# A convolution and a gated unit on one core: where the fourth product of two first stages stands, and how the last stores are cut

## The chip, the cores and the metric

The kernel runs on one core of one Trainium2 chip. The metric is the device time of one execution in microseconds (us), the median of several. A core has TensorE (PE in the profile, its weight loads apart as PEld), VectorE (DVE), ScalarE (ACT), GpSimd (POOL) and SyncE (SP). Each has its own queue of instructions in an order that is fixed when the program is built, and goes on only when the semaphores that its next instruction waits for are there. SP, ACT and POOL also issue the DMAs, which 16 DMA engines of the core carry out.

## What is computed

The input u has 2048 tokens of 448 channels. It is normalised over the channels, and two branches of the result are added to it: a long convolution, whose kernel is made from 256 complex states for each channel and applied by a Fourier transform of length 4096, and a gated unit.

```python
xn = _layernorm(u, axis=-1)
# branch A, for each channel
dt = exp(log_dt); A = -exp(log_A_real) + 1j * A_imag; C = (C_real + 1j * C_imag) * dt
K = 2 * einsum("dn,dnl->dl", C, exp(A * dt * pos)).real
y = irfft(rfft(xn, 4096) * rfft(K, 4096))[:2048] + xn * D_skip
# branch B, F = 1792
h = sigmoid(xn @ w_gate) * (xn @ w_up)
out = u + y + h @ w_down
```

## The kernel before

**Two generators, one order.** `conv()` (branch A) and `glu()` (branch B) are Python generators. A loop at the end of the kernel takes a step of one or of the other by the work that each has announced with `yield`. The instructions so recorded are then put in order by a scheduler that keeps an estimate of each engine's time; `hp` raises a priority, and `tc.issue_after(x)` keeps instructions behind x. So a step that is moved in the source may move its neighbours on all engines.

**The gated unit.** The tokens are worked in two halves of 1024 (`half`), each of two groups of 512 (`t`). The 14 blocks of 128 columns of F go in five groups (`FCH`), in reverse for the second half. For each block and t, `gate` (L695) makes two banks of 128x512 in PSUM, first the gate (i = 0), then the up half (i = 1), 11 matmuls each, since every fp32 product is done as three products of split parts (wh, wl, xh, xl, xr). Between the two halves a step may be called (`between`). ACT takes tanh of the first (th), DVE makes hf from it and the second bank, ACT casts hh, DVE makes the rest hl. When a group's blocks are done, `po` matmuls (L825) multiply by w_down, and DVE adds to `acc` (L830).

**PSUM.** The banks named gu, kq and po share four buffers of the pool `psg`. A product that needs a fifth waits until ACT or DVE has read one of the four.

**The convolution's kernel.** `kgen` makes the chunks of K: POOL makes magnitudes (me, mf), TensorE phases (tr), ACT sines (S), DVE Et and Ft, and TensorE multiplies them in groups of 32 matmuls into `ko` (L616). Ft has one buffer: TensorE's next group waits for DVE's Ft, and DVE's Ft for TensorE's last group. Every fourth chunk a first stage of the transform follows (kp and kq, L566).

**The second half's input, where the change is.** During the last group of the first half (`cross`) the tokens of the second half are loaded, normalised, transposed for the gated unit and put through the first stage of their transform, in four pairs of 128-token blocks (8, 10, 12, 14). The steps are `pair_norm` (L670), `pair_turn` (L675: eight transposes, through `x_transpose`, with xh, xl and xr made from them) and `pair_first` (L681). A pair's first stage is four products, g = 0 to 3, each of two matmuls of 32 rows (`x_first_stage`, L276), each into a gu bank of its own; ACT copies each bank out and stores it to DRAM (`x1_d`) from its own queue. Three lists say when: `mid` between the halves of a gate, `end` behind a gate, `downs` behind a po block:

```python
mid = [(pair_norm, 8), None, (pair_first, 8), (pair_first, 10)]
end = [(), ((pair_turn, 8), (pair_norm, 10)), ((pair_turn, 10), (pair_norm, 12)), ((pair_turn, 12), (pair_norm, 14))]
downs = {(0, 0): (pair_first, 12), (0, 1): (pair_turn, 14), (0, 3): (pair_first, 14)}
```

So pairs 8 and 10 have all four products between the two halves of a gate, which holds one of the four banks for its first half and needs another for its second.

**The end.** `spectra` multiplies the transforms and brings them back; its last step, `last(1, m)`, adds to both channel halves' accumulators in turn, among the last po blocks. H is half of the channels, 224. `out` (L235) stores `nb` blocks of tokens in four DMAs of 32 rows each, over the queues it is given.

Of the kernel before, what the change touches and what calls it, by code (L numbers as in the profile page):

```python
# [11 lines left out]
F32 = mybir.dt.float32  # L12
# [8 lines left out]
D = 448  # L21
# [18 lines left out]
H = D // 2  # L40
# [91 lines left out]
def s4d_glu_kernel(ctx, tc, io):  # L132
    nc = tc.nc
# [47 lines left out]
    psg = ctx.enter_context(tc.tile_pool(name="psg", bufs=1, space=PSUM))  # L181
    pg = ctx.enter_context(tc.tile_pool(name="pg", bufs=1, side="left"))
# [8 lines left out]
    def acc_tile():  # L191
        return pg.tile([128, 4, D], F32, name="acc", bufs=2)
# [37 lines left out]
    accs = [acc_tile() for _ in range(2)]  # L230

    def blocks(t, g, b0, nb):
        return t[g, :, b0 // 8, b0 // 4 % 2, b0 % 4 : b0 % 4 + nb]

    def out(src, b0, nb, ds, engs):  # L235

        for g in range(4):
            eng = engs[g % len(engs)]
            eng.dma_start(blocks(out_t, g, b0, nb)[:, :, ds], src[32 * g : 32 * g + 32, b0 % 4 : b0 % 4 + nb, ds])
# [33 lines left out]
    def row(b, g):  # L273
        return 32 * (b // 4 % 2) + 8 * g + 4 * (b // 8) + b % 4

    def x_first_stage(to, xn, g):  # L276

        s = slice(32 * g, 32 * g + 32)
        for i in range(2):
            nc.tensor.matmul(to[64 * i : 64 * i + 64], wx[s], xn[i][s], start=True, stop=True)  # L280
# [381 lines left out]
    def pair_load(b):  # L662

        xns = [pg.tile([128, D], F32, name="xt", tag=t, bufs=2 * FCH[0]) for t in ("hh", "hl")]
        for i in range(2):
            for g in range(4):
                nc.sync.dma_start(xns[i][32 * g : 32 * g + 32], blocks(x_t, g, b + i, 1)[:, 0])
        return xns
# [9 lines left out]
        with hp(HP):  # L678
            x_transpose(xns, xq[-1], 128 * (b % 4))

    def pair_first(b, xns):  # L681

        x1 = pg.tile([128, 2, D], F32, name="x1", tag="wraw", bufs=1)
        pss = [psg.tile([128, 512], F32, name="gu", bufs=4) for _ in range(4)]
        for g in range(4):
            x_first_stage(pss[g][:, :D], xns, g)
        for g in range(4):
            to = x1[:, g] if g < 2 else pg.tile([128, D], F32, name="x1", tag="rd", bufs=RB)
            nc.scalar.copy(to, pss[g][:, :D])
            r = row(b, g)  # L690
            nc.scalar.dma_start(
                x1_d[:, r : r + 2].rearrange("h i k d -> (i k) h d"), to.rearrange("p (h d) -> p h d", h=2)
            )
# [36 lines left out]
    def glu():  # L730
        for half in range(2):
# [4 lines left out]
            for fs_ in ORDER[half]:  # L736
# [3 lines left out]
                final = half == 1 and fs_ is ORDER[1][-1]  # L740
# [4 lines left out]
                if cross:  # L745
                    xts = {b: pair_load(b) for b in range(8, 16, 2)}
                    step = lambda f_, b: f_(b, xts[b])
                    mid = [(pair_norm, 8), None, (pair_first, 8), (pair_first, 10)]
                    end = [(), ((pair_turn, 8), (pair_norm, 10)), ((pair_turn, 10), (pair_norm, 12)), ((pair_turn, 12), (pair_norm, 14))]
                    downs = {(0, 0): (pair_first, 12), (0, 1): (pair_turn, 14), (0, 3): (pair_first, 14)}  # L750
                for n_, (f, t) in enumerate(order):
                    if t == 0:
# [52 lines left out]
                for t in range(2):  # L805
                    acc = accs[2 * half + t]
                    for b in range(4):
                        if final and (t, b) == (0, 1):

                            yield None  # L810
                        if final and t == 1 and b >= 2:

                            sp_mm[:] = glu_mm
                            for m in (4 * b - 8, 4 * b - 6):
                                lasts[0](1, m)
                            if b == 3:
                                out(accs[2], 8, 4, slice(H, D), (nc.sync, nc.scalar))
                                out(accs[3], 12, 3, slice(0, D), (nc.sync, nc.scalar))
                        po = psg.tile([128, D], F32, name="po", tag="gu", bufs=4)
                        bs = slice(128 * b, 128 * b + 128)  # L820
                        n = 0
                        with tc.issue_after(sp_mm[0].ins) if glu_on else nullcontext():
                            for (hh, hl), (dh, dl) in zip(hs[t], wts):
                                for a_, w_ in ((hh, dh), (hh, dl), (hl, dh)):
                                    glu_mm[:] = [nc.tensor.matmul(  # L825
                                        po, a_[:, bs], w_, start=(n == 0), stop=(n == 3 * fc - 1)
                                    )]
                                    n += 1
                        with hp(HP):
                            v.scalar_tensor_tensor(  # L830
                                acc[:, b], po, 0.5, acc[:, b], ALU.mult, ALU.add
                            )
                        yield 0.6 * fc
                        if cross and (t, b) in downs:
                            step(*downs[t, b])
                    if cross:
                        nc.sync.dma_start(acc_d[:, 4 * t : 4 * t + 4], acc)
                    if final and t == 0:
                        out(acc, 8, 4, slice(0, H), (nc.gpsimd,))
                    elif final:  # L840
                        out(acc, 15, 1, slice(0, D), (nc.sync, nc.scalar))

    def spectra(pf):

# [265 lines left out]
    xq, psc, raws, acl, marks, slots, pqs = list(x_first), [], [], [], [None, None], {}, []  # L1110
    W1s, GGs, act, exps = [], [], [], []
    gens = [conv(), glu()]
    total = [sum(Y0) + 11 * WP + 8 * WX + 34 + NCK * WK + HOLE + 17 * WS, 2 * (4 + NFT * 14.8) - HELD]
    done = [0.0, 0.0]
# [40 lines left out]
```

## Time and profile before

| | us |
|---|---|
| median of three executions | 713.99 |
| lowest, highest | 711.97, 716.0 |
| the profiled execution, another one | 710.54 |
| its span, first to last instruction | 708.8 |

The granted TensorE clock was 0.988 over the span; 1.00 is full speed. Six stretches of the profiled execution matter for reading it (times from the span's start): up to 130 us loads, normalisation and preparation; 130 to 260 the gated unit's first half with the chunks of K; 260 to 335 its last group with the second half's input; to about 525 the second half with the rest of K; to 690 the spectra with the gated unit; from 690 the last blocks and stores.

A row of a timeline has start and length in us, engine, line, operation, output<-inputs, and in brackets the idle time of the engine just before it and what ended that. In a row of windows the busy times of PE, PEld, DVE, ACT and POOL follow the window's length, then the granted clock, the busy share of the DMA engines and GB/s.

### The profile page before, as it was taken

How to read it: one execution, taken by the hardware profiler on the slowest of the kernel's cores; microseconds unless marked ns; L12 is line 12 of the kernel's file. 1: busy time of each engine (PE TensorE's matmuls, PEld its weight loads, DVE VectorE, ACT ScalarE, POOL GpSimd, SP SyncE). 2: the span in 40 equal slices, each digit the busy share in tenths (PEclk: the TensorE clock that was granted, in tenths of full speed). 3: DMA queues.
4: the chain of work that ended last, by engine and by line, in shares of the span. 5: the costliest groups of instructions: out<-in, count | busy, mean ns of one | idle time of the engine just before them, and what ended most of it. 6: DMA issues, size and time to landing. Idle time of an engine off the chain costs nothing. (4 is left out here: it accounts for less than half of the span.)

```text
span 708.8 us, 19098 instructions
## 1 busy us (share of the span) xinstructions
PE 668.1 (94%) x7752; PEld 523.7 (74%) x7752; DVE 555.7 (78%) x766; ACT 428.7 (60%) x678; POOL 384.9 (54%) x433
## 2 busy tenths in 40 slices
PE   2798999999999998999999999999999999999996
PEld 2575878878877875756878878877777777777784
DVE  5899987699899998898478899988946555566544
ACT  3656965578689779877577788778543322322320
POOL 2101227655999999777446698798765001344001
PEclk9999999999999998989999999999999999999999
DMA  9956274554253544546833333242269988999756
GB/s 200 239 149 204 70 230 150 170 183 132 63 169 135 169 123 135 162 146 202 258 112 103 92 112 108 68 138 82 54 179 280 257 236 238 266 272 221 182 146 182
DMA packets 93031, 117.22 MB, mean 165 GB/s; under 512 B 12240, under 2 KB 76624, under 8 KB 92944
## 3 DMA queue, kind: packets, MB, share of 16 engines
q1 hardware_dynamic: 65376, 91.75, 46.3%
q10 hardware_dynamic: 24896, 18.13, 8.7%
q0 software_dynamic: 2672, 6.13, 3.2%
q8 instruction: 61, 1.00, 0.6%
q14 instruction: 26, 0.21, 0.1%
HBM read 72.13 MB, written 43.84 MB: 164 GB/s over the span
## 5 line engine op out<-in xcount | busy, mean ns | idle before, releaser
L520 POOL TENSOR_TENSOR me<-me,pm 128x32 f32<-128x32 f32 (+1 forms) x168 | 154.9, 922 | 66.8 <-DVE Et L603 38.1
L520 POOL TENSOR_TENSOR mf<-mf,pm 128x64 f32<-128x64 f32 (+1 forms) x112 | 116.9, 1044 | 5.1
L709 PE MATMUL gu<-xh,wh 128*128 128x512 f32 x336 | 100.1, 405 | 3.8 <-DVE acc L830 1.6
L709 PE MATMUL gu<-xh,wl 128*128 128x512 f32 x336 | 96.9, 393 | 0.0
L709 PE MATMUL gu<-xl,wh 128*128 128x512 f32 x336 | 95.1, 390 | 0.0
L602 DVE TENSOR_TENSOR Et<-me,S 128x1024 f32<-128x1024 f32 x56 | 80.2, 1433 | 11.6 <-ACT S L551 10.3
L825 PE MATMUL po<-dh,hh 128*128 128x448 f32 x224 | 84.2, 376 | 3.1 <-ACT hh L725 1.9
L548 ACT ACTIVATE S<-tr 128x1024 f32<-128x1024 f32 x56 | 57.7, 1030 | 44.9 <-PE tr L542 41.0
L604 DVE TENSOR_TENSOR Ft<-mf,S 128x1024 f32<-128x1024 f32 x56 | 80.1, 1431 | 5.3 <-PE ko L616 3.7
L603 DVE TENSOR_TENSOR Et<-me,S 128x1024 f32<-128x1024 f32 x56 | 80.4, 1436 | 4.8 <-ACT me L533 4.5
L825 PE MATMUL po<-dh,hl 128*128 128x448 f32 x224 | 82.4, 369 | 0.3 <-DVE hl L727 0.3
L825 PE MATMUL po<-dl,hh 128*128 128x448 f32 x224 | 82.3, 368 | 0.0
L709 PEld LDWEIGHTS gu<-xh,wh 128*128 128x128 f32 x336 | 60.8, 189 | 24.2 <-issue 4.4
L709 PEld LDWEIGHTS gu<-xh,wl 128*128 128x128 f32 x336 | 63.4, 189 | 14.7 <-DVE ve L255 0.7
L709 PEld LDWEIGHTS gu<-xl,wh 128*128 128x128 f32 x336 | 63.0, 188 | 13.5
L725 ACT CAST hh<-hf 128x512 fp32r<-128x512 f32 x56 | 34.9, 623 | 62.4 <-DVE hf L720 61.4
L616 PEld LDWEIGHTS ko<-Et,Ft 128*32 128x32 f32 x3584 | 54.7, 112 | 24.2 <-issue 13.4
L720 DVE SCALAR_TENSOR_TENSOR hf<-th,gu 128x512 f32<-128x512 f32 x56 | 38.1, 680 | 39.9 <-PE gu L709 35.2
L786 POOL TENSOR_TENSOR dl<-rd,dh 128x448 fp32r<-128x448 f32 x14 | 25.6, 1830 | 78.8 <-ACT dh L785 68.5
L616 PE MATMUL ko<-Et,Ft 128*32 128x64 f32 x3584 | 65.2, 223 | 2.6 <-DVE Ft L604 2.4
L551 ACT ACTIVATE S<-S,hpi 128x1024 f32<-128x1024 f32 x56 | 65.5, 1170 | 0.0
L717 ACT ACTIVATE th<-gu 128x512 f32<-128x512 f32 x56 | 33.5, 599 | 49.4 <-PE gu L709 43.0
(208 smaller groups left out, 1318.0 us busy)
## 6 DMA issues: line engine op xcount, KB each, us to landing
sk_d<-sk ACTq DMA_DIRECT2D x14, 512.0 KB
sx<-x_d SPq DMA_DIRECT2D x32, 224.0 KB
skl<-sk_d SPq DMA_DIRECT2D x16, 448.0 KB
vp<-v_d SPq DMA_DIRECT2D x16, 448.0 KB
v_d<-vt SPq DMA_DIRECT2D x14, 448.0 KB
ph<-ph_d SPq DMA_DIRECT2D x224, 24.0 KB
wt_d<-wh SPq DMA_DIRECT2D x9, 512.0 KB
wt_d<-wl SPq DMA_DIRECT2D x9, 512.0 KB
```

Of the source, the lines that this page charges most:

```text
L520: ins = nc.gpsimd.tensor_tensor(m[:, :, w + a : 2 * w : n], m[:, :, a:w:n], par(base + i).unsqueeze(2).to_broadcast([128, 4 * DC, w // n]) ...
L548: nc.scalar.activation(rows(cs), pv, AF.Abs)
L551: sins[:] = [nc.scalar.activation(cs, cs, AF.Sin, scale=-TWO_PI, bias=hpi)]
L602: v.tensor_tensor(Et[:, :, :, 32:64], two(me[:, :, 32:64]), S[:, 1::-1], ALU.mult)
L603: v.tensor_tensor(Et[:, :, :, 0:32], two(me[:, :, 0:32]), S[:, 1:3, :, ::-1], ALU.mult)
L604: fts[:] = [v.tensor_tensor(Ft, two(mf), S[:, 3:5], ALU.mult)]
L616: mm = nc.tensor.matmul(ko[32 * j : 32 * j + 32, sl], Ft[:, cc, DC * h + 4 * q + j], Et[:, cc, DC * h + 4 * q + j], start=(k == 0), stop=( ...
L709: glu_mm[:] = [nc.tensor.matmul(ps, a_, b_, start=(n == 0), stop=(n == len(mm) - 1))]
L717: marks[0] = nc.scalar.activation(th, pgu[0], AF.Tanh, scale=0.5)
L720: marks[1] = v.scalar_tensor_tensor(hf, th, 1.0, pgu[1], ALU.add, ALU.mult)
L725: nc.scalar.copy(hh, hf)
L825: glu_mm[:] = [nc.tensor.matmul(po, a_[:, bs], w_, start=(n == 0), stop=(n == 3 * fc - 1))]
```

## The change

`pair_first` takes a range of products. For pairs 8 and 10 the first three stay between the halves of a gate (`pair_three`), and the fourth (`pair_fourth`) becomes a step behind that gate, ahead of the next pair's transposes. Pairs 12 and 14 are as they were. Of the last stores, blocks 12 and 13 are now stored by channel halves, the first half from POOL's queue behind the po block (1, 1), the second from SP and ACT; blocks 14 and 15 are stored together at the end, where it was blocks 12 to 14 and then 15.

```diff
-    def pair_first(b, xns):
-
-        x1 = pg.tile([128, 2, D], F32, name="x1", tag="wraw", bufs=1)
-        pss = [psg.tile([128, 512], F32, name="gu", bufs=4) for _ in range(4)]
-        for g in range(4):
+    def pair_three(b, xns):
+        pair_first(b, xns, range(3))
+
+    def pair_fourth(b, xns):
+        pair_first(b, xns, range(3, 4))
+
+    def pair_first(b, xns, gs=range(4)):
+
+        if 0 in gs:
+            x1 = pg.tile([128, 2, D], F32, name="x1", tag="wraw", bufs=1)
+        pss = {g: psg.tile([128, 512], F32, name="gu", bufs=4) for g in gs}
+        for g in gs:
             x_first_stage(pss[g][:, :D], xns, g)
-        for g in range(4):
+        for g in gs:
...
-                    mid = [(pair_norm, 8), None, (pair_first, 8), (pair_first, 10)]
-                    end = [(), ((pair_turn, 8), (pair_norm, 10)), ((pair_turn, 10), (pair_norm, 12)), ((pair_turn, 12), (pair_norm, 14))]
+                    mid = [(pair_norm, 8), None, (pair_three, 8), (pair_three, 10)]
+                    end = [
+                        (), ((pair_turn, 8), (pair_norm, 10)),
+                        ((pair_fourth, 8), (pair_turn, 10), (pair_norm, 12)),
+                        ((pair_fourth, 10), (pair_turn, 12), (pair_norm, 14)),
+                    ]
...
-                                out(accs[3], 12, 3, slice(0, D), (nc.sync, nc.scalar))
+                                out(accs[3], 12, 2, slice(H, D), (nc.sync, nc.scalar))
...
+                        if final and (t, b) == (1, 1):
+                            out(acc, 12, 2, slice(0, H), (nc.gpsimd,))
...
-                        out(acc, 15, 1, slice(0, D), (nc.sync, nc.scalar))
+                        out(acc, 14, 2, slice(0, D), (nc.sync, nc.scalar))
```

**TensorE at pair 8's products, before.** The order in which the scheduler put them, from the third product on. gu<-xt,wx are the products, two matmuls each; gu<-ident,xt the transposes; gu with xh, xl, xr the gate; ko<-Et,Ft the chunks of K; tr its phases.

```order
L280 MATMUL gu<-xt,wx 64x448 x4
L213 MATMUL gu<-ident,xt 64x128 x2
L542 MATMUL tr<-sel,ph_1112 128x512 x2
L280 MATMUL gu<-xt,wx 64x448 x2
L616 MATMUL ko<-Et_1104,Ft 32x64 x32
L709 MATMUL gu<-xh,wh 128x512 x3
L709 MATMUL gu<-xr,wh 128x512
L709 MATMUL gu<-xh,wl 128x512 x3
L709 MATMUL gu<-xr,wl 128x512
L709 MATMUL gu<-xl,wh 128x512 x3
```

The same place in the changed kernel, up to the transposes of pair 8's last columns and the gate's second half behind them:

```order
L280 MATMUL gu<-xt,wx 64x448 x4
L213 MATMUL gu<-ident,xt 64x128 x2
L542 MATMUL tr<-sel,ph_1112 128x512 x2
L716 MATMUL gu<-xh,wh 128x512 x3
L716 MATMUL gu<-xr,wh 128x512
L716 MATMUL gu<-xh,wl 128x512 x3
L716 MATMUL gu<-xr,wl 128x512
L716 MATMUL gu<-xl,wh 128x512 x3
```

The fourth product and the ko group have moved behind the gate's second half; the ko group follows it there, among the kp and kq matmuls.

**TensorE at the next gate, before.** Its first half, then pair 10's first two products and the transposes of that pair's last columns:

```order
L709 MATMUL gu<-xh,wh 128x512
L709 MATMUL gu<-xr,wh 128x512
L709 MATMUL gu<-xh,wl 128x512 x3
L709 MATMUL gu<-xr,wl 128x512
L709 MATMUL gu<-xl,wh 128x512 x3
L280 MATMUL gu<-xt,wx 64x448 x4
L213 MATMUL gu<-ident,xt 64x128 x2
```

The changed kernel at the same gate, from pair 8's fourth product on, of which the two matmuls stand apart:

```order
L280 MATMUL gu<-xt,wx 64x448
L213 MATMUL gu<-ident,xt 128x128 x6
L542 MATMUL tr<-sel,ph_1111 128x512 x2
L280 MATMUL gu<-xt,wx 64x448
L616 MATMUL ko<-Et_1105,Ft 32x64 x28
L213 MATMUL gu<-ident,xt 64x128 x2
L616 MATMUL ko<-Et_1105,Ft 32x64 x4
L716 MATMUL gu<-xh,wh 128x512 x3
```

The transposes of pair 10's last columns (64x128), which wait for DVE's xl of the columns before them, were behind the gate's first half and now stand ahead of it.

**SP's last stores.** They stand behind the last loads of vp, before and in the changed kernel (ACT's queue has the same stores):

```order
L951 DMA vp<-v_d 16x32x224
L239 DMA out_dram<-ac 32x4x224 x4
L239 DMA out_dram<-acc 32x4x224 x2
L239 DMA out_dram<-acc 32x1344 x2
L239 DMA out_dram<-acc 32x448 x2
```

```order
L964 DMA vp<-v_d 16x32x224
L239 DMA out_dram<-ac 32x4x224 x4
L239 DMA out_dram<-acc 32x2x224 x2
L239 DMA out_dram<-acc 32x4x224 x2
L239 DMA out_dram<-acc 32x896 x2
```

Each queue still issues ten; the pieces of three whole blocks (32x1344) have become pieces of two blocks' channel halves, and the last pieces are of two blocks instead of one. POOL's queue has one more row of four, 32x2x224.

## The prediction

> **What bounds the kernel now.** I read the page first, then the stages, then TensorE's row of the page by windows.
>
> ```profile
> PE 668.1 (94%) x7752; PEld 523.7 (74%) x7752; DVE 555.7 (78%) x766; ACT 428.7 (60%) x678; POOL 384.9 (54%) x433
> 260.00:340.00 80.00, 74.61 (x1027) 50.30 (x1026) 68.80 (x78) 67.85 (x110) 64.58 (x74) 0.91 0.56 168
> 340.00:410.00 70.00, 69.17 (x1130) 56.46 (x1129) 54.45 (x60) 46.76 (x68) 38.84 (x50) 1.00 0.45 130
> ```
>
> TensorE is busy 94% of the span, and 69.17 of 70 us right behind the changed stage. So what the stage 260 to 340 saves is worth its full size to the end, unless something later waits for another engine. That stage is the kernel's poorest: TensorE idles 5.4 us (80 less 74.61) and has a granted clock of 0.91. The mean hides two stretches at half clock, which I cut out in windows of 3.41 us (columns: length, PE, PEld, DVE, ACT and POOL busy, clock, DMA share, GB/s).
>
> ```profile
> 272.46:275.87 3.41, 2.66 (x73) 1.43 (x73) 3.41 (x6) 2.95 (x7) 3.17 (x5) 1.00 0.19 49
> 275.87:279.28 3.41, 2.16 (x11) 0.68 (x12) 3.41 (x5) 3.41 (x6) 3.33 (x3) 1.00 0.03 7
> 279.28:282.70 3.42, 3.42 (x47) 1.38 (x49) 2.81 (x2) 3.42 (x9) 3.26 (x5) 0.50 0.50 160
> 282.70:286.11 3.41, 3.41 (x42) 2.76 (x32) 1.74 (x2) 3.41 (x6) 3.41 (x6) 0.50 0.54 171
> 286.11:289.52 3.41, 3.41 (x52) 2.43 (x51) 1.97 (x3) 1.79 (x3) 2.72 (x4) 1.00 0.49 162
> 306.59:310.00 3.41, 2.59 (x35) 1.07 (x34) 3.41 (x6) 3.41 (x7) 3.22 (x4) 1.00 0.07 23
> 310.00:313.41 3.41, 3.41 (x49) 1.49 (x48) 3.41 (x5) 3.41 (x7) 3.17 (x4) 0.50 0.60 183
> 313.41:316.83 3.42, 3.42 (x16) 2.51 (x20) 3.32 (x6) 2.25 (x6) 1.57 (x2) 0.50 0.02 5
> ```
>
> Each stretch is two such windows (0.50). Each follows a window with little weight loading (0.68 and 1.07 us), a first slow window with 1.38 or 1.49 us does not end it, and one with 2.5 us or more does. DVE is full in all of the rest (3.41 of 3.41): from 288 on, the stage runs at DVE's pace, and only in the first slow stretch does DVE itself run dry.
>
> **The change: the fourth product of two pairs.** Rows of TensorE first (start, length, then the idle time before), then of DVE, one of ACT last.
>
> ```profile
> 277.98 0.97 PE L280 MATMUL gu<-xt,wx 32*64 32x448 f32 x4 [1.25 <-DVE xl L220]
> 279.97 1.75 PE L280 MATMUL gu<-xt,wx 32*64 32x448 f32 x4
> 281.65 1.93 PE L616 MATMUL ko<-Et,Ft 128*32 128x64 f32 x64
> 283.52 1.65 PE L709 MATMUL gu<-xh,wh 128*128 128x512 f32 x3
> 284.97 0.63 PE L709 MATMUL gu<-xr,wh 128*128 128x512 f32 x1
> 285.39 1.20 PE L709 MATMUL gu<-xh,wl 128*128 128x512 f32 x3
> 293.81 0.85 PE L709 MATMUL gu<-xl,wh 128*128 128x512 f32 x3
> 318.69 0.48 PE L825 MATMUL po<-dh,hh 128*128 128x448 f32 x1
> 323.52 0.54 PE L616 MATMUL ko<-Et,Ft 128*32 128x64 f32 x22 [0.17 <-DVE Ft L604]
> 326.18 0.41 PE L213 MATMUL gu<-ident,xt 128*64 128x128 f32 x2 [0.75 <-DVE xl L223]
> 334.90 0.97 PE L709 MATMUL gu<-xh,wh 128*128 128x512 f32 x3 [0.70 <-DVE acc L830]
> 280.87 1.22 DVE L603 TENSOR_TENSOR Et<-me,S 128x1024 f32<-128x1024 f32 x1
> 283.71 1.32 DVE L604 TENSOR_TENSOR Ft<-mf,S 128x1024 f32<-128x1024 f32 x1 [1.62 <-PE ko L616]
> 287.55 0.69 DVE L720 SCALAR_TENSOR_TENSOR hf<-th,gu 128x512 f32<-128x512 f32 x1 [2.07 <-PE gu L709]
> 289.08 2.35 DVE L602 TENSOR_TENSOR Et<-me,S 128x1024 f32<-128x1024 f32 x2
> 293.09 0.68 DVE L220 TENSOR_TENSOR xl<-gu,xh 128x512 fp32r<-128x512 f32 x1
> 293.69 0.41 DVE L223 TENSOR_TENSOR xl<-gu,xh 128x256 fp32r<-128x256 f32 x1
> 294.02 1.25 DVE L604 TENSOR_TENSOR Ft<-mf,S 128x1024 f32<-128x1024 f32 x1
> 315.13 1.21 DVE L602 TENSOR_TENSOR Et<-me,S 128x1024 f32<-128x1024 f32 x1
> 285.21 0.53 ACT L689 COPY x<-gu 128x448 f32<-128x448 f32 x1
> ```
>
> Pair 8's third product still waits 1.25 us for DVE: the edit leaves it where it was, so that wait stays, and with it the half clock from 279.28. What goes from there is the fourth product (1.75 us) and the ko group (1.93), both at half clock; the gate's second half now starts at 279.97 instead of 283.52. It is dense, so I expect it to end the slow stretch after one window, at 282.70, as the window with 2.76 us of weight loads did. Slow, its matmuls start 0.42 to 0.48 apart (283.52 to 284.97 to 285.39); fast, some 0.23 (three in 0.85, the last one's pass included): six by 282.70 and five more in 1.1, done at 283.8. Were the clock to stay low, at 284.8.
>
> DVE: Et ends at 282.09, then hf waits for the gate until 283.8: 1.7 us idle where there were 1.62 + 2.07 = 3.69. Gain 2.0 (1.0 if the clock stays low).
>
> Behind it a new wait comes in. The transposes of pair 10 that were behind the gate now stand ahead of its first half and need DVE's xl. From Ft (285.35, behind hf 0.6, xt 0.5, xr 0.4) DVE needs 1.32, three Et of 1.17 (two take 2.35) and two xl (1.0): 291.2. TensorE has nothing but 28 ko matmuls until then and stands idle some 2.7 us in front of a whole gate. Yet that gate starts at 291.5 with 32 ko and the transposes done, and DVE's next Ft, at 294.02 before, comes at 291.75: 2.3 ahead. The gate before ended at 294.66, now at 294.05.
>
> From that Ft on DVE is the pace. To the end of the Et at 315.13 it took 22.3 us (294.02 to 316.34); one pm of 0.9 now comes behind that Et and 0.4 more waiting for ACT's S ahead of it, so it ends at 313.6. TensorE needs that Et for its ko group and is through with the transposes and tr in front by about 310.2 (xl at 308.9 and S at 309.6, stepped through the new order): a second new wait, of 3.4 us. The half clock that I expect behind it (313.4 to 316.8) costs nothing, since the next po waits for xr, and a pm, two Et and the xr itself (0.9 + 2.35 + 0.4) are DVE's until 317.3. That po is the row at 318.69: 1.4 ahead. What followed it took until 334.20 (334.90 less 0.70), of which 0.17 + 0.75 = 0.92 idle, behind Ft and xl. Both waits go: the transposes no longer stand behind Ft. Stage: 1.4 + 0.92 = **2.3 us less**. Bounds: 0.1 less (half clock in the gate at 291.5, below) and 3.2 less (the whole lead of 2.3 is kept to that po).
>
> What moves with the fourth product: its copy on ACT (0.53) and its store on ACT's queue. Behind them stand S of the next chunk and the xh casts; DVE comes to those only through its own queue, which is full: nothing, bound 0.5 more. What it stores is read only by the spectra, the last stage. The first-stage buffers (wraw and rd) are free by then. SP's and POOL's queues change by neighbouring swaps; the ks addition comes earlier on POOL: nothing, bound 0.2 either way.
>
> **The stores.** Rows of SP's queue and of stages (share of DMA engines and GB/s last).
>
> ```profile
> 701.12 4.48 SPq L239 DMA_DIRECT2D out_dram<-acc  x6
> 696.00:698.00 2.00, 2.00 (x26) 1.59 (x9) 1.93 (x4) 0.00 (x0) 0.00 (x0) 1.00 0.03 8
> 698.00:700.00 2.00, 2.00 (x66) 1.20 (x65) 1.22 (x3) 0.00 (x0) 0.00 (x0) 1.00 0.77 180
> 702.00:704.00 2.00, 0.09 (x1) 0.00 (x0) 0.62 (x1) 0.00 (x0) 0.00 (x0) 1.00 0.96 263
> 704.00:706.00 2.00, 0.00 (x0) 0.00 (x0) 0.00 (x0) 0.00 (x0) 0.00 (x0) 0.99 1.03 317
> 706.00:708.80 2.80, 0.00 (x0) 0.00 (x0) 0.00 (x0) 0.00 (x0) 0.00 (x0) 0.50 0.22 75
> 702.12 0.62 DVE L830 SCALAR_TENSOR_TENSOR acc<-po,acc 128x448 f32<-128x448 f32 x1 [0.50 <-PE po L825]
> ```
>
> From 698 on the 16 DMA engines are nearly full, until about 706.6 (0.22 of the last 2.8 us). What ends last is bytes, not the last add (702.12 + 0.62 = 702.74). The change takes four pieces of 32x2x224 floats, 229 KB, to POOL some 2 us ahead of that (share 0.03). At 263 to 317 GB/s that is 0.7 to 0.9 less. Against it: they overlap the ac stores by up to half (0.4), and 229 KB of the rest go in rows of 896 B instead of 5376 (180 at share 0.77 is 234 a full share, against 308: 0.2 more). And twice the bytes now wait for the last add: 459 KB at 300 are 1.5 us, from 702.74 to 704.3 at the earliest, so no new bound. I take **0.4 less**, bounds 0.9 less and 0.2 more.
>
> **Sum.** 2.3 + 0.4 = 2.7 us off. The profiled execution took 710.54 (span 708.8), so 707.8 for one like it. The runs' median is 713.99 (711.97 to 716.0): 3.45 above, which one more slow stretch (half of 6.83 us) would explain, though nothing here shows that. Off the median: **711.3**. About 0.5%, 3.6 us, is what a measurement of this kernel can tell from no change.
>
> **A page against the rows.** The Trainium skill, "TensorE: Matmul & The Clock Gate", Part 1, says the clock halves after an idle window of about 3.4 us and is whole again after a busy one. The length and the return agree with this trace (two windows of 3.41 at 0.50). The threshold differs: the longest idle stretch of the window ahead of 279.28 was 1.25 us. By that page the 2.7 us wait ahead of the gate would leave the clock whole and the half-clock rival below would fall; by the rows it may not.
>
> **The rivals.**
> - *More than that, 710.0.* The stage's upper bound (3.2) and the stores' (0.8). For it: DVE paces the region, and a lead of DVE's is kept where nothing takes it. Against: the reordered xr gives part of it back.
> - *The gate runs at half clock, 713.5.* The 2.7 us wait leaves a window at or under 1.07 us of weight loads. The windows at 286.11 and 289.52 would hold some 1.4 each, about the 1.43 at 272.46 that was let pass. Then the gate ends at 296.3, DVE idles 2.2 us, and the stage's gain is 0.1.
> - *Given back later, 713.6.* TensorE waits for POOL in front of the half's last first stage, and POOL's chain of loads there need not come earlier:
>
> ```profile
> PE kp L566 <- POOL ks L627: 2.3, 3, 1.2
> ```
>
>  2.3 us in three waits, 1.2 the longest. Against: POOL itself waits for DVE and TensorE, which come earlier. Only the stores' 0.4 would be left.
> - *Slower, 719.1.* Both new waits (2.7 and 3.4 us) halve the clock for two windows each, since too little dense work follows, as at 279.28 and 310.00, and the first stretch doesn't end early. Stage 1.3 less, 2 x 3.41 us more, stores 0.4 less: 5.1 more. It decides where the window behind the wait holds under some 1.5 us of weight loads. Against: a gate follows the first wait.
>
> **Chances.** Forecast 0.45 (own range 709.5 to 713), more 0.17, half clock 0.20, given back 0.08, slower 0.10. Faster by over 0.5% (under 710.4): 0.14 of the second and 0.16 of the first, 0.30. Slower (over 717.6): 0.10 and 0.01 for a surprise. The rest, 0.59, is within. The range, 708.8 to 715.8, takes in all but the slower case and the ends of the others.
>
> **What would show it.** Right: in the profile after, the gate behind pair 8's third product starts about 280, clock 1.00 from 282.7, an idle stretch of 2 to 3 us named for DVE's xl in front of the next gate, another for Et near 310 to 314, and po's row of 318.69 about 1.4 earlier, and the DMA engines, busy until 3.9 us behind the last add, end 0.4 sooner behind it. Wrong: half clock in the gate behind the first new wait, or a wait for POOL near 525 that has grown by what the stage saved.

## The result and the profile after

The changed kernel took 717.42 us (median of 14 runs, 714.36 to 719.92), the kernel before 712.52 us beside it (14 runs, 710.10 to 716.50). The ratio is 1.0059, 95% interval [1.0037, 1.0082]: slower by 0.6%, where 711.3 us was forecast. The profiled execution took 714.91 us (span 713.1; before 710.54 and 708.8).

Where it went is read from instructions that both profiles have: how late does the same one come? Three places on DVE first, before the change (start, length): an Ft ahead of the changed stage, the last adds to `acc` of the first half, the first two of the second half's second group.

```profile
256.05 1.32 DVE L604 TENSOR_TENSOR Ft<-mf,S 128x1024 f32<-128x1024 f32 x1
334.76 1.14 DVE L830 SCALAR_TENSOR_TENSOR acc<-po,acc 128x448 f32<-128x448 f32 x2
449.24 1.14 DVE L830 SCALAR_TENSOR_TENSOR acc<-po,acc 128x448 f32<-128x448 f32 x2
```

The same after the change, with the very last add behind them:

```profile
255.73 1.33 DVE L604 TENSOR_TENSOR Ft<-mf,S 128x1024 f32<-128x1024 f32 x1
335.93 0.62 DVE L841 SCALAR_TENSOR_TENSOR acc<-po,acc 128x448 f32<-128x448 f32 x1 [1.88 <-PE po L836]
453.48 1.15 DVE L841 SCALAR_TENSOR_TENSOR acc<-po,acc 128x448 f32<-128x448 f32 x2
707.20 0.62 DVE L841 SCALAR_TENSOR_TENSOR acc<-po,acc 128x448 f32<-128x448 f32 x1 [0.50 <-PE po L836]
```

The Ft is 0.3 early. The first half's last add ends at 336.55 instead of 335.90, 0.65 late: **the stage lost 1.0 us**. The adds of 449.24 are 4.24 late: **the seam**, from the end of the first half to there, **lost 3.6**. The last add (702.12 before) is 5.08 late: 0.8 more was lost later. The span ends 4.3 later, so 0.8 came back behind the last add. The table further down splits every run so, from the start times of those four adds and of the Ft.

**The stage.** Windows on the grid on which the clock changed in this execution (columns as in the prediction):

```profile
276.60:280.01 3.41, 2.32 (x12) 1.41 (x13) 3.41 (x5) 3.41 (x7) 3.41 (x3) 1.00 0.21 70
280.01:283.42 3.41, 3.41 (x90) 2.67 (x92) 3.18 (x5) 3.41 (x7) 3.25 (x6) 1.00 0.54 171
286.84:290.25 3.41, 1.50 (x59) 0.86 (x58) 3.41 (x5) 3.41 (x7) 3.41 (x3) 0.99 0.93 303
290.25:293.66 3.41, 3.41 (x16) 2.39 (x17) 2.81 (x3) 3.02 (x6) 3.33 (x3) 0.51 0.26 82
310.73:314.14 3.41, 1.14 (x4) 0.44 (x4) 3.41 (x4) 3.41 (x7) 3.25 (x3) 0.99 0.27 68
314.14:317.56 3.42, 2.88 (x33) 2.55 (x34) 3.42 (x4) 2.90 (x6) 3.10 (x2) 0.50 0.61 201
317.56:320.97 3.41, 3.41 (x23) 2.22 (x23) 2.94 (x5) 2.77 (x6) 2.18 (x5) 0.51 0.00 0
```

The old slow stretch at 279 is absent, and both new waits halve the clock: for one window behind the first, for two behind the second. TensorE's rows, with two of DVE at the end:

```profile
277.69 0.97 PE L280 MATMUL gu<-xt,wx 32*64 32x448 f32 x4 [1.25 <-DVE xl L220]
279.29 0.86 PE L716 MATMUL gu<-xh,wh 128*128 128x512 f32 x3
290.22 0.64 PE L213 MATMUL gu<-ident,xt 128*64 128x128 f32 x2 [1.92 <-DVE xl L223]
291.16 1.65 PE L716 MATMUL gu<-xh,wh 128*128 128x512 f32 x3
295.02 0.97 PE L280 MATMUL gu<-xt,wx 32*64 32x448 f32 x4
314.68 1.07 PE L616 MATMUL ko<-Et,Ft 128*32 128x64 f32 x28 [2.29 <-DVE Et L602]
320.61 0.61 PE L836 MATMUL po<-dh,hh 128*128 128x448 f32 x1
335.73 0.84 PE L716 MATMUL gu<-xh,wh 128*128 128x512 f32 x3
338.32 0.63 PE L616 MATMUL ko<-Et,Ft 128*32 128x64 f32 x26
291.30 1.23 DVE L604 TENSOR_TENSOR Ft<-mf,S 128x1024 f32<-128x1024 f32 x1 [0.54 <-PE ko L616]
313.41 1.21 DVE L602 TENSOR_TENSOR Et<-me,S 128x1024 f32<-128x1024 f32 x1
```

The second half's gate starts at 335.73 (334.90 before), and ko work of 0.63 us that used to stand ahead of it now stands behind its first half (26 records, two to a matmul, as the 64 of a group of 32 show).

**The seam.** ACT's rows at that place, before and then after (ACTq: its queue of DMAs):

```profile
335.56 0.41 ACT L457 ACTIVATE pm<-W,one 128x128 f32<-128x128 f32 x1
341.03 0.62 ACT L725 CAST hh<-hf 128x512 fp32r<-128x512 f32 x1 [1.03 <-DVE hf L720]
344.86 2.45 ACTq L243 DMA_DIRECT2D acc<-in_A_u_dram  x4
347.40 0.60 ACT L717 ACTIVATE th<-gu 128x512 f32<-128x512 f32 x1 [5.75 <-DMA acc<-in_A_u_dram]
```

```profile
346.18 2.11 ACTq L243 DMA_DIRECT2D acc<-in_A_u_dram  x3
348.33 0.62 ACT L732 CAST hh<-hf 128x512 fp32r<-128x512 f32 x1 [8.75 <-issue]
352.98 0.42 ACT L457 ACTIVATE pm<-W,one 128x128 f32<-128x128 f32 x1
```

ACT loads the second half's `acc` into the buffer of the first half's, and may issue that only when SP's store of the old `acc` has landed (at 346.12 in the profile after, 338.72 and 7.40 in the row further down; the loads go at 346.18). In both kernels it stands there, 5.75 and 8.75 us. Before, the cast hh, the powers (pm) and S were ahead and only a tanh behind; now hh, S and the powers are behind. What that did, on DVE and on TensorE (the first row is the same hl before the change):

```profile
341.68 0.69 DVE L727 TENSOR_TENSOR hl<-hf,hh 128x512 fp32r<-128x512 f32 x1 [0.69 <-DMA dh<-dt_d]
348.99 0.69 DVE L734 TENSOR_TENSOR hl<-hf,hh 128x512 fp32r<-128x512 f32 x1 [5.42 <-ACT hh L732]
349.60 1.22 DVE L604 TENSOR_TENSOR Ft<-mf,S 128x1024 f32<-128x1024 f32 x1
364.02 2.08 DVE L604 TENSOR_TENSOR Ft<-mf,S 128x1024 f32<-128x1024 f32 x1
359.15 1.10 PE L616 MATMUL ko<-Et,Ft 128*32 128x64 f32 x64 [1.30 <-DVE Ft L604]
366.15 1.10 PE L616 MATMUL ko<-Et,Ft 128*32 128x64 f32 x64 [1.20 <-DVE Ft L604]
```

DVE stands 5.42 us at hl, with Ft queued behind it, and TensorE then waits 2.5 us for Ft where it waited for nothing between 340 and 372. POOL, which stood 13.12 us for the powers, has a part in the second of these waits: the Ft of 364.02 took 2.08 us beside POOL's late magnitudes (others took 1.22). How much is POOL's, these rows do not split. The other 1.1 of the 3.6 is put down to work left over: the ko (0.63) and a tr of that size behind the gate; two executions without a wait of TensorE there, e7 and e14 below, lost 1.1 and 1.0. The store is even a piece of the chain that ended last, and TensorE is busy 67.16 of the 70 us that held 69.17:

```profile
338.72 7.40 DMA acc_d<-acc
```

```profile
340.00:410.00 70.00, 67.16 (x1005) 55.10 (x1004) 57.60 (x62) 48.17 (x70) 48.05 (x51) 1.00 0.46 137
```

**Behind 410** all is 4.2 us late and stays so until 650. There TensorE waits 1.06 us for DVE, one of whose additions ran beside POOL's dl and took 1.21 us (rows of TensorE, DVE, POOL). Between 449 and the last add other profiles lost -0.1 to 1.4, the most of them e11, without pair 8's move; so this loss is not tied to that product.

```profile
650.16 0.96 PE L975 MATMUL pv<-vp,wf 64*32 64x224 f32 x16 [1.06 <-DVE pd L927]
647.74 1.21 DVE L929 TENSOR_TENSOR yy<-pd 128x224 f32<-128x224 f32 x1
647.53 1.17 POOL L805 TENSOR_TENSOR dl<-rdw,dh 128x448 fp32r<-128x448 f32 x1
```

**The end.** SP's last stores, then the windows around the last add, which ends at 707.82 (last columns: share of the DMA engines, GB/s):

```profile
705.66 3.83 SPq L239 DMA_DIRECT2D out_dram<-acc  x6
```

```profile
706.00:708.00 2.00, 1.16 (x6) 0.74 (x4) 1.32 (x3) 0.00 (x0) 0.00 (x0) 1.00 0.85 257
708.00:710.00 2.00, 0.00 (x0) 0.00 (x0) 0.00 (x0) 0.00 (x0) 0.00 (x0) 1.00 0.89 233
710.00:713.10 3.10, 0.00 (x0) 0.00 (x0) 0.00 (x0) 0.00 (x0) 0.00 (x0) 0.51 0.40 146
```

The DMA engines are again nearly full until about 711.2 (0.40 of the last 3.1 us), 3.4 us behind the last add where it was 3.9, and the span ends 5.3 us behind the last add (713.1 less 707.82); before it was 6.1 (708.8 less 702.74).

### The profile page after: what moved, and what is told of

It is laid out like the page before. It is cut to its first block, busy times and chain, and to the rows that moved or that the text cites. A ratio compares the mean times of both kernels' runs of the same rounds, so it can differ in the third digit from the quotient of the medians.

```text
span 713.1 us, 19103 instructions
## 1 busy us (share of the span) xinstructions
PE 670.1 (94%) x7752; PEld 525.6 (74%) x7752; DVE 560.8 (79%) x766; ACT 428.4 (60%) x678; POOL 400.9 (56%) x437
## 4 chain that ended last, share of the span: by engine, by line
PE 61%; DVE 12%; issue 9%; DMA 8%; ACT 4%; SPq 2%; POOL 2%; ACTq 0%; DVEq 0%; POOLq 0%
PE gu L716 23%; PE po L836 15%; PE sp L915 7%; PE ko L616 5%; PE pv L942 4%; PE tr L542 3%; DVE Ft L604 3%; DVE Et L603 2%; DVE Et L602 2%; DMA xe<-in_A_u_dram 1%; DMA aim<-in_A_A_imag_dram 1%; DMA acc_d<-acc 1%; DVE pm L454 1%; PE pv L975 1%; POOL dl L797 1%
## 5 line engine op out<-in xcount | busy, mean ns | idle before, releaser
L520 POOL TENSOR_TENSOR mf<-mf,pm 128x64 f32<-128x64 f32 (+1 forms) x112 | 127.3, 1136 | 4.9
L604 DVE TENSOR_TENSOR Ft<-mf,S 128x1024 f32<-128x1024 f32 x56 | 83.7, 1494 | 9.9 <-PE ko L616 6.6
L603 DVE TENSOR_TENSOR Et<-me,S 128x1024 f32<-128x1024 f32 x56 | 83.9, 1499 | 6.6 <-ACT me L533 6.0
L602 DVE TENSOR_TENSOR Et<-me,S 128x1024 f32<-128x1024 f32 x56 | 79.2, 1415 | 11.7 <-ACT S L551 9.3
L841 DVE SCALAR_TENSOR_TENSOR acc<-po,acc 128x448 f32<-128x448 f32 x80 | 48.2, 616 | 21.5 <-PE po L836 21.5
L734 DVE TENSOR_TENSOR hl<-hf,hh 128x512 fp32r<-128x512 f32 x56 | 47.1, 842 | 18.2 <-ACT hh L732 18.2
```

The source lines that it names most:

```text
L520: ins = nc.gpsimd.tensor_tensor(m[:, :, w + a : 2 * w : n], m[:, :, a:w:n], par(base + i).unsqueeze(2).to_broadcast([128, 4 * DC, w // n]) ...
L602: v.tensor_tensor(Et[:, :, :, 32:64], two(me[:, :, 32:64]), S[:, 1::-1], ALU.mult)
L603: v.tensor_tensor(Et[:, :, :, 0:32], two(me[:, :, 0:32]), S[:, 1:3, :, ::-1], ALU.mult)
L604: fts[:] = [v.tensor_tensor(Ft, two(mf), S[:, 3:5], ALU.mult)]
L734: v.tensor_tensor(hl, hf, hh, ALU.subtract)
L841: v.scalar_tensor_tensor(acc[:, b], po, 0.5, acc[:, b], ALU.mult, ALU.add)
```

## The experiments

All ratios are to the kernel before on the same chip, with 95% intervals. "Stage" and "seam" are the losses of the one profiled execution against the profile before. One execution's stage scatters by several us (-1.0 to +7.1 with pair 8's product moved), so it is read in the mean only.

| run | ratio | stage | seam |
|---|---|---|---|
| the change | 1.0059 [1.0037, 1.0082] | +1.0 | +3.6 |
| e1 stores alone | 0.9968 [0.9942, 0.9994] | +2.3 | 0.0 |
| e2 both pairs alone | 1.0074 [1.0045, 1.0103] | +2.7 | +3.9 |
| e3 pair 8 alone | 1.0071 [1.0044, 1.0097] | -1.0 | +3.7 |
| e4 pair 10 alone | 0.9992 [0.9971, 1.0012] | -0.2 | +0.4 |
| e5 change, ko of two chunks first | 1.0042 [1.0019, 1.0065] | +3.9 | +1.1 |
| e6 change, ko of one chunk first | 1.0063 [1.0038, 1.0088] | +4.6 | +4.5 |
| e7 change, loads from POOL | 1.0030 [1.0008, 1.0053] | +3.2 | +1.1 |
| e8 before, ko of two chunks first | 1.0004 [0.9982, 1.0027] | +0.5 | +0.3 |
| e9 change, first wait filled | 1.0069 [1.0041, 1.0097] | +0.9 | +5.0 |
| e10 change, e5 and e7 together | 1.0022 [0.9997, 1.0047] | +5.6 | -0.3 |
| e11 stores and pair 10 | 0.9961 [0.9935, 0.9987] | -1.7 | +0.1 |
| e12 stores, loads from POOL | 0.9981 [0.9948, 1.0013] | -0.6 | +0.1 |
| e13 change, transposes first | 1.0010 [0.9981, 1.0039] | +2.0 | -0.4 |
| e14 the change again | 719.24 us, one run | +7.1 | +1.0 |
| e15 the change again | 718.11 us, one run | +3.2 | +4.4 |

### The parts one by one: e1 to e4

My theory was that the two parts add, that the loss lies in the moved products, and there in the order at the seam; the rivals, that the stores lose, or that each moved product costs its own wait.

e1 has of the change only the hunks on `out`. 

> The kernel before with the cut of the last stores alone; no product is moved. Theory (the two parts add, and the loss lies in the first): the stores gain what the two profiles show behind the last add, 6.06 less 5.25, so 0.8 us, and the wait of 0.94 us near 650 in the profile after is a coincidence of later work: ratio 0.999, 711.7 against 712.5, DMA engines idle about 5.2 us behind the last add. Rival (the stores are the loss): 1.003 to 1.006, with the 0.94 us wait here too. Rival (nothing at all from stores): 1.000, about 6.0 us behind the last add.

Measured 0.9968, 711.24 us: the stores gain. Behind the last add its span has 5.1 us left; near 650 TensorE waits 0.28 us, where it was 1.06 in the profile after. Over all profiles here this tail is 4.9 to 5.7 us with the cut stores (12 of them, 5.2 in the mean) and 6.0 to 6.1 without (5): 0.8 us, as expected. The rest of the 2.3 us that the ratio shows is within the interval.

e2 has only the hunks on the pairs. 

> The change without its cut of the stores: the fourth products of pairs 8 and 10 alone. Theory: the whole loss and 0.8 us more, ratio 1.007, some 717.5 to 718; DVE's Ft of 330.5 in the profile before about 8 late, PE's later work 4 to 5 late. Rival (the stores are the loss): 1.000 to 1.002.

Measured 1.0074, 718.5 us: the whole loss. Without the stores' gain it should be somewhat more than the change's; it is, but the two intervals overlap.

e3 moves pair 8's fourth product alone, on the kernel before (the helpers as in the change; only the entries that differ are shown):

```diff
-mid = [(pair_norm, 8), None, (pair_first, 8), (pair_first, 10)]
+mid = [(pair_norm, 8), None, (pair_three, 8), (pair_first, 10)]
-       ((pair_turn, 10), (pair_norm, 12)),
+       ((pair_fourth, 8), (pair_turn, 10), (pair_norm, 12)),
```

> The kernel before with the fourth product of pair 8 alone behind its gate; pair 10 keeps all four between the halves; stores as before. In this kernel's order ACT's powers (pm) stand behind the loads of acc, as in the changed kernel. Theory (order at the seam of the two halves costs most: ACT waits at the loads of acc with the powers behind them, POOL's magnitudes start some 17 late, TensorE goes short near 350 to 370): most of the loss, ratio 1.004 to 1.007, 715.5 to 717.5. Rival (each moved product costs its own wait and half clock, alike): half of it, 1.003, 714.7. Rival (pair 10's part is the loss): 1.000.

Measured 1.0071, 718.57 us: all of it, more than my range. Its profiled execution, the fastest of the seven (713.92), gained 1.0 in the stage and still lost 3.7 at the seam.

e4 does the same with pair 10 alone (`pair_three` at 10, `pair_fourth` at 10 ahead of `pair_turn` at 12). 

> The kernel before with the fourth product of pair 10 alone behind its gate; pair 8 keeps all four; stores as before. In this kernel's order ACT's powers stay ahead of the last loads of acc, as before the change. Theory (order at the seam): within 0.2% of before, 0.998 to 1.002, 711 to 714; POOL's magnitudes at about 336 as before. Rival (each moved product costs its own wait and half clock): 1.003, 714.7.

Measured 0.9992, 712.47 us: nothing. So it is not moving a product that costs, nor two products half each. It is pair 8's, and with it comes the other order at the seam.

### The seam: e5 to e8

Theory: ACT's powers behind the loads of `acc` make POOL late. e5 leaves the change whole and raises the priority of two chunks' ko, which brings the old order back (arguments shortened):

```diff
+with hp(HP) if cn in (26, 27) else nullcontext():
     mm = nc.tensor.matmul(ko[...], Ft[...], Et[...], ...)
```

> The changed kernel, stores and both pairs included, with a raised priority for the ko matmuls of two chunks (the 27th and 28th) and nothing else: their order now has that whole ko work and the next tr ahead of the second half's first gate, and ACT's powers (pm) ahead of the loads of acc, as before the change. Theory (the products' move itself is harmless, the loss is the order that it left at the seam of the two halves): POOL's magnitudes begin at about 336 to 340 where they began at 353.5, TensorE's idle time of 350 to 370 goes, and the time is 3.6 to 4.5 us less than the changed kernel's: 712.9 to 713.8, ratio 0.999 to 1.002. Rival (the new waits and their half clock in the stage are the loss): no better than 1.004, since both products stay where the change put them.

Measured 1.0042, 715.45 us. The seam lost 1.1 instead of 3.6, but the time fell only to the edge between the two theories, and its interval overlaps the change's: this execution lost 3.9 in the stage. POOL's magnitudes begin at 340.3, as expected; TensorE's waits did not all go, it still stands 1.30 us for Ft at 360.5. ACT still stood 8.44 us at the loads, now with only S behind them:

```profile
352.34 1.76 ACTq L243 DMA_DIRECT2D acc<-in_A_u_dram  x4
354.15 1.03 ACT L548 ACTIVATE S<-tr 128x1024 f32<-128x1024 f32 x1 [8.44 <-issue]
```

e6 has `cn in (27,)`. 

> The changed kernel with that priority for the 28th chunk's ko alone: the ko rest that stood behind the second half's first gate now stands ahead of it, but the next tr still behind the second gate, and ACT's powers still behind the loads of acc. Theory (the powers behind the loads make POOL late): hardly better than the changed kernel, 1.004 to 1.006, POOL's magnitudes still after 350. Rival (the ko rest and DVE's Ft behind it are what is late): most of it comes back, 0.999 to 1.002.

Measured 1.0063, 718.62 us, seam 4.5, POOL's magnitudes at 356.4: as the theory has it. Bringing the ko rest ahead of the gate is not enough while S and the powers stay behind the loads; here hh was ahead.

e7 moves the loads to another queue:

```diff
-x_load(accs[q], 4 * q, 4, [nc.scalar])
+x_load(accs[q], 4 * q, 4, [nc.gpsimd])
```

> The changed kernel with the second half's loads of acc issued from POOL's queue, ahead of its next magnitudes, instead of ACT's: ACT's 8.75 us of standing at these loads goes. Theory (in this order the powers stand behind S of a tr that stands behind the first gates on TensorE, so they come as late without the loads): POOL's magnitudes still begin after 350, 1.004 to 1.006. Rival (ACT standing at the loads is the whole cause): they begin at about 345, 0.999 to 1.002.

Measured 1.0030, 715.85 us, seam 1.1. My theory foresaw POOL's part; the median lies between the two theories and the interval reaches into both, so the trace has to decide. POOL's rows, then DVE's:

```profile
349.51 2.00 POOL L243 DMA_DIRECT2D acc<-in_A_u_dram  x4 [6.04 <-DMA acc_d<-acc]
352.02 0.28 POOL L520 TENSOR_TENSOR me<-me,pm 128x32 f32<-128x32 f32 x1 [0.51 <-ACT pm L457]
```

```profile
347.37 0.69 DVE L734 TENSOR_TENSOR hl<-hf,hh 128x512 fp32r<-128x512 f32 x1 [0.69 <-ACT hh L732]
349.09 1.23 DVE L604 TENSOR_TENSOR Ft<-mf,S 128x1024 f32<-128x1024 f32 x1 [1.02 <-PE ko L616]
```

POOL's magnitudes begin at 352.0, as late as I said, and yet 2.5 us came back at the seam: TensorE shows no wait between 338 and 376, and DVE's 5.42 us at hl are 0.69. The last add of the first half ends at 339.64 here, at 339.71 in e15 and 339.61 in e2, where the seam lost 4.4 and 3.9: so it is not a late stage that hides the loss. The powers are only one of the things that may not stand behind the loads. ACT's stand is the cause, and what it holds up and for how long sets the price. With hh, S and powers behind the loads it was 3.6 to 5.0 in five profiles (the change, e2, e3, e9, e15) and 1.0 in a sixth (e14, read below), with S and powers 4.5 (e6), with S alone 1.1 (e5), with a tanh 0 (before). In the change, e2, e3 and e9 that is two waits of TensorE for Ft, 2.4 to 2.7 us together; in e15 and e6 it is one, of 1.8 and 2.1, with a window at half clock behind it. e5 and e6 are one profile each, so the order of these prices is not firm.

The Trainium skill, "DMA: Bandwidth & Descriptors", section "Issuing engines are not separate DMA queues", says that issuing from several engines saves only the time of the issue, usually small. The Trainium skill's next section there, "Two DMAs through the same engine are not ordered", has the issuing engine wait on the first DMA's semaphore before it issues a dependent one. Here the issue of three loads took 2.11 us, and the engine stood 8.75: on a compute engine that wait, not the issue, was the price.

e8 is the control: e5's edit on the kernel before. 

> A control: the kernel before with the same raised priority for the ko matmuls of the two chunks. Its order at the seam was good already (powers ahead of the loads, the ko work ahead of the gate). Theory: no change, 0.998 to 1.002, so that what the priority gives the changed kernel is the repair of the order. Rival (the priority is a gain whatever the order): about 0.995, as much off as it takes off the changed kernel.

Measured 1.0004, 712.79 us: the priority by itself gives nothing.

### What is left: e9 and e10

e9 puts ten matmuls (20 records in the profile) where the first new wait was:

```diff
+if k == 3 and fill:      # fill: b == 10
+    fp = psc[-1].tile([128, 512], F32, name="kp", bufs=1)
+    for _ in range(10):
+        nc.tensor.matmul(fp[:, :128], ident, ident, start=True, stop=True)
```

> The changed kernel with ten extra matmuls (128x128 with the identity, into a bank that nobody reads) on TensorE ahead of pair 10's last two transposes, where the first new wait stood; they add work that the result doesn't need. ACT's powers stay behind the loads of acc, as in the changed kernel. Theory (the new wait's price in the stage is the half clock behind it: one window of 3.41 us in the gate, some 1.3 us): the gate behind the transposes runs at 1.00 and the time is 1 to 2 us less than the changed kernel's, 1.002 to 1.005 of before, in spite of 2 us of added work. Rival (the wait itself is the price, the clock is not): no better than the changed kernel, 1.006 or more.

Measured 1.0069, 717.77 us: no better, the rival's number. The gate behind the transposes did run at full speed, its first three matmuls in 0.97 us where they took 1.65:

```profile
290.08 2.50 PE L214 MATMUL kp<-ident 128*128 128x128 f32 x20
294.79 0.97 PE L720 MATMUL gu<-xh,wh 128*128 128x512 f32 x3
```

But the fill took 2.5 us itself, and the gate started 3.6 later than in the profile after, in an execution that also had a slow window at 278.9. The stage lost 0.9 in this execution and the seam 5.0, so the median does not tell what the fill did. This doesn't separate the clock from the wait, and it is no repair.

e10 joins e5 and e7. 

> The changed kernel with both repairs of the seam: the raised priority for the two chunks' ko, and the loads of acc from POOL's queue. Theory (two losses, one at the seam from ACT standing at the loads of acc, some 3.6 us in the changed kernel and 1.0 with either repair, and one in the stage itself, some 1 to 4): from the last add of the first half to 410 nothing more is lost than before the change, the stage's loss stays, less what the stores gain: 1.000 to 1.003. Rival (all the loss is at the seam): 0.997, as with the stores alone.

Measured 1.0022, 714.19 us, seam -0.3, no wait of TensorE there. The theory holds: the seam's loss is gone, and the stage's stays. Against the stores alone (0.9968) that is 0.5%, some 3.8 us.

### Versions that keep what gains: e11 and e12

e11 is the cut of the stores with pair 10's product moved and pair 8's not. 

> The cut of the stores with pair 10's fourth product moved, pair 8 as before the change: the two parts that lost nothing by themselves (0.9968 and 0.9992). Theory: they add, 0.995 to 0.998, 709 to 711. Rival (what the stores gave was luck of the runs): 0.999 to 1.001.

Measured 0.9961, 709.4 us: faster than both kernels, and 1% faster than the change; from e1 alone (0.9968) it is not to be told apart.

e12 is e1 with e7's edit. 

> The cut of the stores alone with the loads of acc from POOL's queue; no product is moved. In the profile before ACT also stands at these loads, 5.75 us, with only casts and a tanh behind it, since powers and S are ahead. Theory (standing there costs only when S and the powers are behind it): the same as the stores alone, 0.996 to 0.998. Rival (it costs wherever it stands): another 2 to 3 us off, 0.993 to 0.994.

Measured 0.9981, 711.82 us, with an interval from 0.9948 to 1.0013: no sign of the rival's 2 to 3 us more. Where only a tanh stands behind the loads, ACT's stand there costs nothing that can be measured.

### The stage: e13 to e15

e13 turns two steps round:

```diff
-((pair_fourth, 8), (pair_turn, 10), (pair_norm, 12)),
-((pair_fourth, 10), (pair_turn, 12), (pair_norm, 14)),
+((pair_turn, 10), (pair_fourth, 8), (pair_norm, 12)),
+((pair_turn, 12), (pair_fourth, 10), (pair_norm, 14)),
```

> The changed kernel with the order of two steps behind a gate turned round: the next pair's transposes first, then the fourth product. In its order all six of pair 10's wide transposes stand behind 32 ko matmuls, and ACT's powers stand ahead of the last four loads of acc, though behind a tanh. Theory (stage and seam both come from the order): the seam loses 0 to 1, the stage 0 to 1, less the stores: 0.997 to 1.001. Rival (any move of pair 8's product costs): 1.004 or more, as in the kernels with pair 8 moved.

Measured 1.0010, 713.33 us: within the theory's range by the median ratio, with the seam's loss gone; the stage lost 2.0, more than the 0 to 1 that it allowed. The interval reaches from the one theory almost to the other.

> The changed kernel itself, one more execution with a profile. Theory: seam again 3.5 to 4 lost (an order, the same each time); stage anywhere from 1 gained to 5 lost, by how many half-clock windows fall into it. Rival (the seam's loss was a coincidence of one execution too): a seam's loss outside 3 to 5.

> As e14, a third execution of the changed kernel with a profile: seam 3.5 to 4 lost, the stage free between 1 gained and 5 lost with the time at half clock in it.

e15 came near what was expected (seam 4.4, a little above 3.5 to 4; stage 3.2). e14 did not: stage 7.1, seam 1.0, both outside the range that I gave, and the seam as the rival had it. Two windows at half clock (331.4 to 338.2) helped to make its stage late. At the seam ACT stands in the same order, but for a shorter time, and so does DVE:

```profile
351.74 0.62 ACT L732 CAST hh<-hf 128x512 fp32r<-128x512 f32 x1 [5.31 <-issue]
352.39 0.69 DVE L734 TENSOR_TENSOR hl<-hf,hh 128x512 fp32r<-128x512 f32 x1 [1.97 <-ACT hh L732]
```

SP issued the store of the old `acc` at 343.41, 0.03 us behind the last add; in the profile after it issued it 2.2 us behind (336.55 to 338.72), with loads of dh ahead of it on its queue. TensorE then shows no wait between 336 and 412. So the order brought the stand in all three executions, but not the same price: it was lower where the store went out sooner, and TensorE did not feel it there. Stage and seam together are 8.2 in e14, 7.6 in e15 and 4.6 in the first.

With pair 8's product moved (nine profiles, without e9 and e13) the stage lost 3.4 in the mean; without (six) 0.05. TensorE's idle time in it was 7.5 against 5.3, its busy time 75.1 against 74.0, the time at half clock about the same (14.0 and 13.1). So most of that loss is idle time: the new waits, which are not paid back. How much of the rest is the clock stays open.

## Why the prediction was wrong

- **The third product's wait and the gate behind it: right.** The wait is 1.25 us again, and the gate's second half moved from 283.52 to 279.29 (279.97 forecast). What was said to stay "with it", the half clock from 279.28, did not come here, and came in others: in e15, with the same program, the window that ends at 278.73 held 1.29 us of weight loads and the next ran at half clock, while here 1.41 in the window up to 280.01 let it pass.

```profile
275.32:278.73 3.41, 2.16 (x72) 1.29 (x72) 3.41 (x4) 3.41 (x6) 3.33 (x2) 0.99 0.07 20
278.73:282.15 3.42, 3.42 (x10) 1.70 (x9) 3.42 (x4) 3.42 (x7) 3.42 (x4) 0.50 0.39 137
```

- **The first new wait: right in place, kind and effect on DVE.** 1.92 us for xl ahead of a gate that started at 291.16 (291.5 forecast), DVE's Ft at 291.30 (291.75). But the gate ran at half clock up to 293.66 and ended at 295.02, which was the rival given 0.20; it happened in eight of the nine profiles with pair 8's product moved as in the change, all but e2. TensorE was busy 1.50 us in the window before that. The Trainium skill, "TensorE: Matmul & The Clock Gate", Part 1, asks for an idle window, by which the clock would have stayed whole; the runs decide against it.
- **The second new wait: its price failed, and with it the stage.** The Et ended at 314.62 instead of 313.6, and "the half clock that I expect behind it (313.4 to 316.8) costs nothing" was wrong: it lasted two windows, to 320.97, and the po that should have started at 317.3 started at 320.61. So DVE's lead of 2.7 us at 291 was gone by then: the stage lost 1.0 here and 3.4 in the mean, where 2.3 of gain stood in the sum. The condition of the slower rival (too little dense work behind the wait) was met behind this one; I gave that rival 0.10.
- **"SP's and POOL's queues change by neighbouring swaps" was true, and the queue that mattered was not among them.** ACT's own order changed at the seam, hh, S and powers against the loads of `acc`, and it stood written in the order before the run. This is 3.6 us in the profile after (4.4 and 1.0 in the two others of the same program) that no term and no rival named: "given back later" put the place at a first stage near 525, on POOL; the place was 340 to 366, on ACT.
- **The stage's gain passes to the end, TensorE being full: right for the loss.** 4.24 late at 449 and 4.1 to 4.2 until 640.
- **The stores: right in kind, sized too low.** 0.4 was forecast with bounds to 0.9; 0.8 is what the tails show. By the sign that was named, the end of the DMA engines' busy stretch behind the last add, it is 0.5 here (3.4 against 3.9 us).
- The 0.8 us between 449 and the last add were in no term; other profiles lose -0.1 to 1.4 there, with and without pair 8's move.

## What to carry to other kernels

When a step is moved, read the new order of every queue to the point where the two orders meet again, the DMA issues too: an issue that must wait for another DMA holds up all that stands behind it on its engine, so look what that is before and after. A lead that is gained ahead of a wait is worth only what the next wait leaves of it; follow it to the end of the stage. And try the parts of a change apart: here one gained, one was free, and the third cost twice what the first gave.

## What was not expected of the hardware

The windows in which the granted clock halves have a fixed length (3.41 us) and another phase against the program in each execution: the same program had the stage's first slow stretch at 278.73 in e15 and none there in the profile after. The Trainium skill, "TensorE: Matmul & The Clock Gate", Part 1, calls the window free-running, and the traces agree. One kernel's times scatter along with the clock: the changed kernel's runs had mean clocks of 0.992 (714.36 us) to 0.976 (719.4).

A window need not be idle to be followed by half clock: those before it held up to 2.16 us of matmuls in the rows shown here, and 2.59 in the prediction's row at 306.59. The weight loads in them, 0.44 to 1.29 us, tell these rows apart better, but they are no rule: e13 had a window with 1.47 that was followed by half clock, and the profile after has one with 1.12, TensorE busy throughout, that was followed by full clock:

```profile
324.38:327.80 3.42, 3.42 (x20) 1.12 (x21) 2.00 (x4) 1.68 (x4) 0.42 (x2) 1.00 0.69 270
```

DVE's addition of 128x224 took 1.21 us beside POOL's dl and 0.39 before the change, where it ran ahead of it. The Trainium skill, "SBUF — State Buffer", "Who interferes with whom", has it that a VectorE instruction with two inputs in SBUF contends with a GpSimd instruction that reads SBUF; these rows agree.
